# An attention and MLP kernel on one core: each attention unit's preparation written one unit ahead, with a third buffer slot for its loads

## The chip, the cores and the metric

The kernel runs on one core of a Trainium2 chip. The metric is the device time of one execution in microseconds (us). The engines are named as the profile names them: PE is TensorE (matmuls; PEld are its weight loads), DVE is VectorE, ACT is ScalarE, POOL is GpSimd, SP is SyncE, which computes nothing and issues every DMA of this kernel from one in-order queue.

## What is computed

Four batches, eight heads, 576 tokens, head width 64. Each head's output mixes causal softmax attention with a read from a memory matrix, and all heads together feed a two-layer MLP with a squared ReLU:

```python
scores = scale * np.matmul(q, k.transpose(0, 1, 3, 2))      # causal mask, softmax -> a
local = np.matmul(a, v)
q_p = np.where(q > 0, q, np.exp(q) - 1.0) + 1.0
mem_out = einsum(q_p, M_prev) / (einsum(q_p, z_prev)[..., None] + 1e-06)
x = g * mem_out + (1 - g) * local                            # (2304, 512)
r = np.maximum(x @ w_in, 0.0)                                # w_in (512, 2048)
return (r * r) @ w_out                                       # w_out (2048, 512)
```

## The kernel before

**Tiles and units.** The 576 tokens of a batch are one tile of 64 and four of 128 (tiles 1 to 4). Tile 0 of every batch is done first, by `first_tokens`. The rest is 24 attention units (line 999): a unit is a batch, a pair of heads and a list of tiles. Units 0 to 3 are tiles 1 and 2 of batch 0, units 4 to 7 its tiles 3 and 4; 8 to 11 and 12 to 15 are the same for batch 1; units 16 to 19 and 20 to 23 are all four tiles of batches 2 and 3. Within a unit the tiles go in the order 2, 1, 3, 4 (`TORD`).

**A unit's front** (lines 440 to 537). From three loads, `kd` (k), `qm` (the memory matrix and q) and `vv` (v), it makes, from unit 6 on, the high and low halves of q and k (`qh`, `ql`, `kh`, `kl`: ACT line 444 and 450, DVE 445 and 451, POOL for early `kl`); phi of q in place in `qm` (ACT 461 and 466, DVE 467); from unit 3 on, a power-of-two scale of v (`vx` line 483, a small matmul `vt` line 487, `vy`) and with it v's halves `vs` (ACT 498, DVE 500); and the memory products `pm` (PE 520), which DVE turns into the first part of the unit's output `feat` (531).

**A unit's rows** (lines 541 to 665). For each tile: scores `sp` (PE 554, three terms by two heads), masked minimum (DVE 575), exponential (ACT 595), the halves `a` of the weights (ACT 633, DVE 635), their transposition `aT` (a DMA on SP's queue, 639), the products with `vs` into `acc` (PE 659), and the scaled sum onto `feat` (DVE 662).

**Loads.** `loads` (414) allocates `kd`, `qm` and `vv` from tags with two buffers each (`KB`, `QB`, `VVB`). `after()`, called between a unit's front and its rows (539), loads the next unit. So a load is held until the unit two before has let go of its buffer.

**MLP blocks.** `moe(n)` for block 0 (the four 64-token tiles) and then for blocks of 256 tokens: block 1 and 2 are batch 0, 3 and 4 batch 1, 5 and 6 batch 2; the two of batch 3 go through `moe_last` at the end. A block is eight steps of 24 matmuls `up` (lines 936 to 938, 256 columns each), squared ReLU and halves (`r`, `gh`, `gl`: ACT 942 to 945, DVE 948) and 12 matmuls `oacc` (908 to 910, 512 columns each). It can start when the four units with its tiles have finished, and their tokens have been split (`hl`) and transposed into `xT` (DMA, 694).

**What sets the order.** The program text is written in the order of `ORD` (line 88): units 0 to 3 merged with the weights' conversion and MLP block 0, then units 4 to 23, then the other MLP blocks. A scheduler then lays the instructions out, engine by engine, and prefers what was written earlier among what it takes to be ready; MLP matmuls, written last, fill what attention leaves on PE. What comes out is a fixed in-order list for each engine. Tiles of one tag share that tag's buffers, and a PSUM tag (`av`, two buffers) is shared by `vt`, `pm` and `acc`.

Of the kernel before, what the change touches and what calls it, by code (L numbers as in the profile page):

```python
# [8 lines left out]
F32 = mybir.dt.float32  # L9
# [9 lines left out]
B, H, S, D = 4, 8, 576, 64  # L19
# [3 lines left out]
P = 128  # L23
# [6 lines left out]
SQ = S - D  # L30
# [11 lines left out]
NEF = 3  # L42
NES = 6
PXT = 'av'
PXE = 'aa'
PHI = 1
QB = 2
VVB = 2
ZW = D + 1
MW = 576  # L50
NRAW = 8
# [8 lines left out]
EB = 3  # L60
EB2 = 3
RB = 2
KB = 2
XB = 3
SEQ = 'a0 g a1 r r c0 l r r c1'
W0 = 9
# [2 lines left out]
NEARLY = 12  # L69
# [11 lines left out]
FIRST = 4  # L81
# [18 lines left out]
def fused_kernel(ctx: ExitStack, tc: tile.TileContext, t0_d, kk_d, qv_d, beta, w_in, w_out, out):  # L100
# [5 lines left out]
    at = atx.enter_context(tc.tile_pool(name="at", bufs=1, side="right"))  # L106
# [26 lines left out]
    def load_beta():  # L133
        nc.sync.dma_start(gpm, beta)
        gates()
# [123 lines left out]
    more = []  # L259
# [12 lines left out]
    def ahead():  # L272
        if len(loaded) < NU:
            load_weight(len(loaded))
            loaded.append(1)
# [16 lines left out]
    def weights():  # L292
        with tc.tile_pool(name="rw", bufs=1) as rw:
            more.append(rw)
            with tc.tile_pool(name="tp", bufs=1, reuse_waits="tile") as tp:
                first_tokens(tp, ahead)
            yield
            yield from pieces(0, NR0, NRAW)
        wpl.append(ctx.enter_context(tc.tile_pool(name="wpl2", bufs=1, reuse_waits="tile")))
        with tc.tile_pool(name="rw2", bufs=1, reuse_waits="tile") as rw:  # L300
            more.append(rw)
            yield from pieces(NR0, NU, NRAW2)
        more.append(ltx.enter_context(tc.tile_pool(name="late", bufs=1, reuse_waits="tile")))
        yield

    def first_tokens(tp, ahead):
# [8 lines left out]
        for step in SEQ.split():  # L315
            if step == "r":
                ahead()
            elif step == "l":
                nxt.append(loads(*order[0]))
            elif step == "g":  # L320
                load_beta()
            else:
                g = int(step[1])
                c0, c1 = {"a": (0, TA), "q": (0, GD), "k": (GD, TA), "c": (TA, TW)}[step[0]]
                nc.sync.dma_start(tr[g][:, c0:c1], t0_d[g, :, c0:c1])
# [85 lines left out]

    feat = {}

    def loads(b, p, tiles):
        qa, qb = QT[tiles[0]][0], sum(QT[tiles[-1]])
        kd = at.tile([P, S], F32, tag="kd", name="kd", bufs=KB)
        nc.sync.dma_start(kd[:, :qb], kk_d[b, p, :, :qb])
        qm = at.tile([P, 2 * ZW + SQ], F32, tag="qm", name="qm", bufs=QB)
        qa, qb = qa - D + 2 * ZW, qb - D + 2 * ZW
        for c0, c1 in [(0, qb)] if qa == 2 * ZW else [(0, 2 * ZW), (qa, qb)]:  # L420
            nc.sync.dma_start(qm[:, c0:c1], qv_d[b, p, :, c0:c1])
        vv = at.tile([P, 5 * P], F32, tag="vv", name="vv", bufs=VVB)
        nv = (tiles[-1] + 1) * P
        nc.sync.dma_start(vv[:, :nv], qv_d[b, p, :, SQ + 2 * ZW : SQ + 2 * ZW + nv])
        return kd, qm, vv

    def attention(b, p, tiles, ld, after, early, sfull, full, ap):
        q_eng, k_eng = (nc.gpsimd if c == 'p' else nc.vector for c in (EARLY if early else LATE))
        late = 0 if early else 1
        h0 = 2 * p  # L430
# [3 lines left out]
        kd, qm, vv = ld  # L434
# [102 lines left out]
            yield  # L537

        after()
        started, a12 = set(), None  # L540
        row = {}

# [43 lines left out]
        for i in [t for t in TORD if t in tiles]:  # L586
            q0, n = QT[i]
# [112 lines left out]
    def prefetch(b, blk):  # L700
        n = blocks.index((b, blk))
        if n < NBLK - 2:
            xT = mo.tile([P, 2, 2 * NK, P], F16, tag="xT", name="xT", bufs=2)
            osc = mo.tile([P, 2], F32, tag="osc", name="osc", bufs=2)
            xq[n] = xT, osc
            token_halves(b, blk, [xT[:, t] for t in range(2)], osc)
            return
# [279 lines left out]
    def need(n):  # L987
        while wn[0] < n:
            next(wg)
            wn[0] += 1  # L990
# [8 lines left out]
    order = []  # L999
# [3 lines left out]
    nxt = []  # L1003
    need(1)
    if not nxt:
        nxt.append(loads(*order[0]))

    def attn(i0, i1):
        for i in range(i0, i1):
            ld = nxt.pop()  # L1010

            def after():
                if i + 1 < len(order):
                    nxt.append(loads(*order[i + 1]))

            yield from attention(*order[i], ld, after, i < NEARLY, i < NES, i < NEF and max(order[i][2]) < 4, more[-1] if i > FIRST and i % 2 else at)
            b, p, tiles = order[i]
            if p == NP - 1:
                need(NU + 2)
                for blk in range(2):  # L1020
                    if 2 * blk + 1 in tiles and b < B - 1:
                        prefetch(b, blk)
                yield

    def na(t):
        return NP * (6 + (len(t) > 3) + 2 * len(t) - 1)

    ORD(merge, attn, na, wsteps, lambda: moe(0), order)
    tl = last_pool()
    for _ in chain(*[moe(n) for n in range(1, NBLK - 2)], moe_last(tl)):  # L1030
# [55 lines left out]
```

## Time and profile before

| what | us |
|---|---|
| median of 3 runs (lowest to highest) | 586.88 (583.03 to 589.49) |
| the profiled execution | 584.98 |
| its span, first to last instruction | 583.2 |
| PE busy in the span | 535.7 (92%) |
| DVE busy | 455.7 (78%) |
| ACT busy | 397.2 (68%) |
| SP's hardware DMA queue, share of 16 DMA engines | 50.6% |

The profile gives each engine's busy time, the idle time ahead of an instruction, and which event ended it. A PE instruction's duration holds its way through the array, so matmuls overlap and their cadence is read from start to start. Idle time of an engine that is not the bound costs nothing by itself.

### The profile page before, as it was taken

To read this page: it belongs to the slowest core of one execution; us is meant where nothing else is said; L and a number is where in the kernel's file an instruction comes from. 1 tells how busy PE (TensorE), PEld (TensorE's weight loads), DVE (VectorE), ACT (ScalarE), POOL (GpSimd) and SP (SyncE) were. 2 spreads that over 40 slices of the span, in tenths; PEclk is the share of its full clock that TensorE was granted. 3 is DMA by queue.
4 is the path that set the end of the run, shared out by engine and by line. 5 is a ranking of instruction groups with operands and counts; after the bars stand their busy time and mean duration, and the time that the engine had idled before them with its cause. 6 is when DMAs were issued, how large, how long until landed. Compare 5 with 4: busy or idle time off the path is not lost.

```text
span 583.2 us, 12895 instructions
## 1 busy us (share of the span) xinstructions
PE 535.7 (92%) x4903; PEld 380.4 (65%) x4903; DVE 455.7 (78%) x1413; ACT 397.2 (68%) x853; POOL 59.7 (10%) x41
## 2 busy tenths in 40 slices
PE   6578997799799899999998999988999999999997
PEld 6466774576577576657765766656676776446766
DVE  6988779998687686889895775989767769795735
ACT  2566886777688677869787866889566664556452
POOL 2760674010010000000000000000000000000000
PEclk9968998699999999999998999999999999999999
DMA  8921886345865643767546846569454335100002
GB/s 308 404 89 38 281 320 164 90 100 121 157 128 117 143 118 91 158 136 174 123 108 104 196 74 118 117 122 178 64 114 86 79 57 71 38 0 1 2 1 72
DMA packets 131022, 70.87 MB, mean 122 GB/s; under 512 B 113296, under 2 KB 119440, under 8 KB 130960
## 3 DMA queue, kind: packets, MB, share of 16 engines
q1 hardware_dynamic: 130960, 70.05, 50.6%
q8 instruction: 38, 0.62, 0.5%
q14 instruction: 24, 0.20, 0.1%
HBM read 37.53 MB, written 4.72 MB: 72 GB/s over the span
## 4 chain that ended last, share of the span: by engine, by line
PE 35%; DVE 21%; ACT 12%; DMA 10%; issue 4%; SPq 1%; POOLq 0%; DVEq 0%; ACTq 0%
DVE a L635 4%; PE oacc L909 4%; PE oacc L908 4%; PE oacc L910 4%; PE up L938 4%; PE up L936 4%; PE up L937 4%; DMA qm<-in_qv_dram 3%; DVE e L575 3%; ACT e L595 3%; DMA vv<-in_qv_dram 3%; PE seven L811 3%; DMA aT<-a 3%; PE acc L659 3%; PE sp L554 2%
## 5 line engine op out<-in xcount | busy, mean ns | idle before, releaser
L936 PE MATMUL up<-xT,w 128*128 128x256 f16 x448 | 123.1, 275 | 1.2 <-ACT r L942 1.2
L937 PE MATMUL up<-xT,w 128*128 128x256 f16 x448 | 123.1, 275 | 0.3 <-DVE xT L397 0.3
L938 PE MATMUL up<-xT,w 128*128 128x256 f16 x448 | 123.2, 275 | 0.0
L595 ACT ACTIVATE e<-e,mx 128x320 f32<-128x320 f32 (+3 forms) x128 | 77.4, 606 | 46.3 <-DVE feat L662 27.4
L908 PE MATMUL oacc<-w,gh 128*128 128x512 f16 x224 | 85.5, 382 | 2.2 <-ACT gh L945 2.1
L635 DVE SCALAR_TENSOR_TENSOR a<-e,a 128x128 f16<-128x128 f32 x116 | 64.8, 569 | 27.3 <-ACT a L633 26.4
L909 PE MATMUL oacc<-w,gh 128*128 128x512 f16 x224 | 85.4, 381 | 0.0
L910 PE MATMUL oacc<-w,gl 128*128 128x512 f16 x224 | 81.0, 380 | 1.3 <-DVE gl L948 1.2
L633 ACT ACTIVATE a<-e 128x128 f16<-128x128 f32 x116 | 54.9, 523 | 3.9 <-DMA aT<-a 2.4
L659 PE MATMUL acc<-vs,aT 128*128 128x64 f16 x1138 | 46.3, 195 | 11.7 <-DMA aT<-a 7.2
L659 PEld LDWEIGHTS <-aT 128*128 128x128 f16 x1138 | 41.5, 99 | 20.8 <-DMA aT<-a 10.2
L937 PEld LDWEIGHTS <-w 128*128 128x128 f16 x448 | 44.3, 99 | 11.5 <-issue 1.5
L938 PEld LDWEIGHTS <-w 128*128 128x128 f16 x448 | 44.2, 99 | 9.2 <-issue 1.2
L936 PEld LDWEIGHTS <-w 128*128 128x128 f16 x448 | 44.2, 99 | 9.2
L575 DVE CUSTOM_DVE_ANT_0 e<-sp,mask 128x320 f32<-128x320 f32 (+3 forms) x128 | 47.0, 417 | 1.5 <-PE sp L554 1.0
L193 POOL TENSOR_SCALAR raw<-raw 128x512 uint32<-128x512 uint16 x21 | 44.8, 2134 | 21.4 <-DMA raw<-in_w_in_dram 12.8
L948 DVE TENSOR_TENSOR gl<-r,gh 128x512 f16<-128x512 f32 x56 | 39.4, 704 | 7.3 <-ACT gh L945 6.9
L942 ACT ACTIVATE r<-up,gam 128x512 f32<-128x512 f32 x48 | 32.3, 674 | 18.2 <-PE up L938 18.2
L910 PEld LDWEIGHTS <-gl 128*128 128x128 f16 x224 | 21.4, 98 | 23.5 <-DVE gl L948 3.4
L811 PEld LDWEIGHTS <-g 128*128 128x128 f16 x336 | 32.6, 98 | 6.0 <-DVE g L737 1.8
L908 PEld LDWEIGHTS <-gh 128*128 128x128 f16 x224 | 22.0, 98 | 22.1 <-ACT gh L945 2.7
L943 ACT ACTIVATE r<-r 128x512 f32<-128x512 f32 x56 | 34.9, 624 | 0.8
(196 smaller groups left out, 1076.1 us busy)
## 6 DMA issues: line engine op xcount, KB each, us to landing
raw<-in_w_in_dram SPq DMA_DIRECT2D x16, 512.0 KB, 7.1
raw<-in_w_out_dram SPq DMA_DIRECT2D x16, 512.0 KB, 7.9
vv<-in_qv_dram SPq DMA_DIRECT2D x16, 320.0 KB, 3.2
kd<-in_kk_dram SPq DMA_DIRECT2D x16, 288.0 KB, 3.2
out_dram<-o SPq DMA_DIRECT2D x12, 256.0 KB, 2.4
qm<-in_qv_dram SPq DMA_DIRECT2D x8, 321.0 KB, 3.4
qm<-in_qv_dram SPq DMA_DIRECT2D x8, 193.0 KB, 2.9
vv<-in_qv_dram SPq DMA_DIRECT2D x8, 192.0 KB, 4.7
```

Of the source, the lines that this page charges most:

```text
L575: nc.vector.tensor_tensor_reduce(out=e[:, h, ka:kb], in0=sps[:, h, cs], in1=mask[:, 448 - q0 + ka : 448 - q0 + kb], scale=-0.125, scalar=3 ...
L595: ex = nc.scalar.activation(e[:n, h, :ke], e[:n, h, :ke], AF.Exp, bias=bs, scale=-1.0, accum_out=sm[:n, h : h + 1])
L633: nc.scalar.mul(av[:, :, o0 : o0 + w], x, SC)
L635: nc.vector.scalar_tensor_tensor(out=av[:, :, o0 + w : o0 + 2 * w], in0=x, scalar=SC, in1=av[:, :, o0 : o0 + w], op0=ALU.mult, op1=ALU.sub ...
L659: nc.tensor.matmul(acc[:n, h], lhs[:, :n], rhs, start=x == 0, stop=x == len(mms) - 1)
L811: mms.append(nc.tensor.matmul(x[:, blk], g[j][:, i0, a, blk, p], t_side(j, p, m, i1), start=j == js[0] and p == n == 0, stop=j == js[-1] a ...
L908: nc.tensor.matmul(acc[t], gh[:, u, ts], w_out_op(f, 0), start=f == f0, stop=False)
L909: nc.tensor.matmul(acc[t], gh[:, u, ts], w_out_op(f, 1), start=False, stop=False)
L910: nc.tensor.matmul(acc[t], gl[:, u, ts], w_out_op(f, 0), start=False, stop=f == f1)
L936: nc.tensor.matmul(up[:, u, :], w_in_op(f, k, 0), xT[:, :, k], start=k == 0, stop=False)
L937: nc.tensor.matmul(up[:, u, :], w_in_op(f, k, 0), xT[:, :, NK + k], start=False, stop=False)
L938: nc.tensor.matmul(up[:, u, :], w_in_op(f, k, 1), xT[:, :, k], start=False, stop=k == NK - 1)
```

## The change

Nothing is computed otherwise; every engine has the same instructions. Three things move.

First, `attention` gets a stop: after a unit's front and its `after()` it yields the word `whole`. `attn` now writes, from unit `FIRST` = 4 on, the front of unit i+1 ahead of the rows of unit i. Second, `loads` names its buffers by slot: unit i uses slot i mod 2 below unit 8 (`AHEAD`) and i mod 3 from there on, each slot its own tag with one buffer; the third slot lies in the pool `more[-1]`. Third, `after()` of unit i loads up to unit i+1, and from unit 6 on up to unit i+2.

```diff
-QB = 2
-VVB = 2
-KB = 2
+AHEAD = 8
-    def loads(b, p, tiles):
+    def loads(i):
+        b, p, tiles = order[i]
+        n = i % 2 if i < AHEAD else i % 3
+        lp = at if n < 2 else more[-1]
-        kd = at.tile([P, S], F32, tag="kd", name="kd", bufs=KB)
+        kd = lp.tile([P, S], F32, tag=f"kd{n}", name="kd")
-        qm = at.tile([P, 2 * ZW + SQ], F32, tag="qm", name="qm", bufs=QB)
+        qm = lp.tile([P, 2 * ZW + SQ], F32, tag=f"qm{n}", name="qm")
-        vv = at.tile([P, 5 * P], F32, tag="vv", name="vv", bufs=VVB)
+        vv = lp.tile([P, 5 * P], F32, tag=f"vv{n}", name="vv")
...
         after()
+        if ap_early:
+            yield "whole"
...
+    def unit(i):
+        ld = nxt.pop(0)
+        def after():
+            while i + len(nxt) + 1 < min(len(order), i + (3 if i + 2 >= AHEAD else 2)):
+                nxt.append(loads(i + len(nxt) + 1))
+        ap = more[-1] if i > FIRST and i % 2 else at
+        early = i < NEF and max(order[i][2]) < 4
+        return attention(*order[i], ld, after, i < NEARLY, i < NES, early, ap, i >= FIRST)
     def attn(i0, i1):
+        ahead = []
         for i in range(i0, i1):
-            ld = nxt.pop()
-            def after():
-                if i + 1 < len(order):
-                    nxt.append(loads(*order[i + 1]))
-            yield from attention(*order[i], ld, after, i < NEARLY, i < NES, i < NEF and max(order[i][2]) < 4, more[-1] if i > FIRST and i % 2 else at)
+            rows = ahead.pop() if ahead else unit(i)
+            if i >= FIRST:
+                for x in (rows,) if i == FIRST else ():
+                    for _ in iter(lambda: next(x), "whole"):
+                        yield
+                if i + 1 < i1:
+                    ahead.append(unit(i + 1))
+                    for _ in iter(lambda: next(ahead[0]), "whole"):
+                        yield
+            yield from rows
```

What the scheduler makes of it is shown at two places; names carry the program's numbers, which differ between the two kernels, and the changed kernel's lines are 2 or 4 apart from the old ones.

SP's queue around the load of unit 11's `qm` and `vv`, before. Here `qm_2495` and `vv_2497` are unit 11's, `aT_2410` is unit 9's and `aT_2525` unit 10's transposition, `kd_2894` is unit 14's:

```order
L639 DMA_TRANSPOSE aT_2410<-a_2409 128x6x128
L417 DMA kd_2894<-in_kk_dram 128x576
L639 DMA_TRANSPOSE aT_2525<-a_2524 128x10x128
L421 DMA qm_2495<-in_qv_dram 128x386
L639 DMA_TRANSPOSE aT_2525<-a_2524 128x6x128
L424 DMA vv_2497<-in_qv_dram 128x384
```

The same two loads now, as `qm_2311` and `vv_2313`; `aT_2217` is unit 7's last transposition, `aT_2341` is unit 8's, `kd_2656` is unit 13's:

```order
L643 DMA_TRANSPOSE aT_2217<-a_2216 128x18x128
L643 DMA_TRANSPOSE aT_2341<-a_2340 128x10x128
L643 DMA_TRANSPOSE aT_2341<-a_2340 128x6x128
L423 DMA qm_2311<-in_qv_dram 128x386
L426 DMA vv_2313<-in_qv_dram 128x384
L419 DMA kd_2656<-in_kk_dram 128x576
```

Unit 11's q and v stood among unit 10's transpositions; they now stand behind unit 8's, two units earlier. The loads of units 12 to 23 have moved by one to two units in the same way.

PE around the first `up` matmul of MLP block 5 (the first block of batch 2, which needs tiles 1 and 2 of units 16 to 19), before. `oacc_6371` is block 4's last sum, the two `pm` are unit 20's memory products, `up_6666` is the new block's first tile:

```order
L910 LDWEIGHTS gl_6631
L910 MATMUL oacc_6371<-w31_1407,gl_6631 128x512
L520 MATMUL pm_4326<-qm_4071 128x130 x2
L520 MATMUL pm_4333<-qm_4071 128x130 x2
L936 LDWEIGHTS w0_522
L936 MATMUL up_6666<-xT_4260,w0_522 128x256
```

And now, where `up_6604` is a step of block 4:

```order
L941 MATMUL up_6604<-xT_3366,w27_1354 128x256
L942 LDWEIGHTS w27_1354
L942 MATMUL up_6604<-xT_3366,w27_1354 128x256
L940 LDWEIGHTS w0_522
L940 MATMUL up_6666<-xT_4314,w0_522 128x256
```

Before, block 4 had run out, down to its last `oacc`, when block 5 began; between unit 19's last product of tile 1 and this matmul PE had 7 `up` and 24 `oacc` matmuls. Now block 4 still has steps to go, and between the same two points stand 96 `up` and 37 `oacc` matmuls.

## Rows read from the trace of the kernel before

**Rows 1.** Busy time by stretch: length, then PE, PEld, DVE, ACT, POOL, clock, DMA.

```profile
134.00:480.00 346.00, 327.10 (x3199) 232.76 (x3197) 269.00 (x966) 255.51 (x585) 3.93 (x4) 1.00 0.60 121
165.00:279.00 114.00, 108.61 (x1024) 77.03 (x1022) 90.38 (x323) 87.29 (x204) 1.87 (x2) 1.00 0.63 137
279.00:441.00 162.00, 152.78 (x1506) 108.98 (x1506) 126.27 (x470) 123.22 (x284) 0.00 (x0) 0.99 0.61 118
480.00:573.00 93.00, 92.04 (x597) 57.91 (x596) 65.39 (x93) 48.32 (x62) 0.00 (x0) 1.00 0.10 18
```

**Rows 2.** Waits of PE, 134 to 480: us in total, times, longest.

```profile
PE acc L659 <- DMA aT<-a: 7.2, 5, 2.8
PE sp L554 <- DVE ql L445: 3.0, 3, 2.3
PE up L936 <- ACT r L942: 1.0, 1, 1.0
```

**Rows 3.** Timeline, unit 11's q: start, us, instruction, and idle before with releaser.

```profile
196.54 0.61 PE L520 MATMUL pm<-qm 128*128 128x130 f32 x4
...
199.49 0.65 SPq L421 DMA_DIRECT2D qm<-in_qv_dram  x1
...
203.43 0.41 PE L554 MATMUL sp<-kh,qh 64*128 64x320 f32 x2 [2.30 <-DVE ql L445]
```

**Rows 4.** Timeline of PE, start to start of neighbouring matmuls.

```profile
377.39 0.27 PE L938 MATMUL up<-xT,w 128*128 128x256 f16 x1
377.50 0.38 PE L908 MATMUL oacc<-w,gh 128*128 128x512 f16 x1
377.72 0.38 PE L909 MATMUL oacc<-w,gh 128*128 128x512 f16 x1
```

**Rows 5.** Timeline of PE, where it stood idle, and unit 17's tile 3.

```profile
147.34 0.99 PE L659 MATMUL acc<-vs,aT 128*128 128x64 f16 x28 [1.22 <-DMA aT<-a]
...
156.85 0.20 PE L659 MATMUL acc<-vs,aT 128*128 128x64 f16 x1 [1.89 <-DMA aT<-a]
...
312.49 1.73 PE L659 MATMUL acc<-vs,aT 128*128 128x64 f16 x29 [2.75 <-DMA aT<-a]
...
335.55 1.62 PE L659 MATMUL acc<-vs,aT 128*128 128x64 f16 x50
...
384.68 0.39 PE L908 MATMUL oacc<-w,gh 128*128 128x512 f16 x1 [1.57 <-ACT gh L945]
...
386.47 0.22 PE L487 MATMUL vt<-identb,vx 128*128 128x128 bf16 x1 [0.74 <-DVE feat L662]
...
405.67 0.99 PE L659 MATMUL acc<-vs,aT 128*128 128x64 f16 x28 [1.57 <-DVE mx L575]
...
450.97 1.63 PE L659 MATMUL acc<-vs,aT 128*128 128x64 f16 x50 [1.16 <-DMA aT<-a]
```

**Rows 6.** SP's transposition for unit 17's tile 3, and all transpositions of line 639.

```profile
330.44 1.51 SPq L639 DMA_TRANSPOSE aT<-a  x1
...
DMA to landing us min/median/max: 2.7/4.1/6.7
```

**Rows 7.** Waits of DVE, 279 to 441.

```profile
DVE vx L483 <- DMA vv<-in_qv_dram: 7.9, 4, 3.0
```

**Rows 8.** Timeline: block 2's tokens on SP, and the block's first `up` on PE.

```profile
186.99 2.72 SPq L694 DMA_TRANSPOSE xT<-hl  x2
...
193.78 0.27 PE L936 MATMUL up<-xT,w 128*128 128x256 f16 x1
```

**Rows 9.** Waits of DVE, 165 to 279.

```profile
DVE ql L445 <- ACT qh L444: 5.2, 4, 2.0
DVE vx L483 <- DMA vv<-in_qv_dram: 4.8, 5, 1.4
```

**Rows 10.** Timeline: unit 10's transposition on SP, and its products on PE.

```profile
198.07 1.33 SPq L639 DMA_TRANSPOSE aT<-a  x1
...
213.53 0.22 PE L659 MATMUL acc<-vs,aT 128*128 128x64 f16 x2
```

More of the change, by code (lines that the diff above doesn't have):

```diff
@@ L318, in first_tokens @@
             elif step == "l":
-                nxt.append(loads(*order[0]))
+                nxt.append(loads(0))
             elif step == "g":
@@ L425, in loads, with attention @@
         return kd, qm, vv
-    def attention(b, p, tiles, ld, after, early, sfull, full, ap):
+    def attention(b, p, tiles, ld, after, early, sfull, full, ap, ap_early):
         q_eng, k_eng = (nc.gpsimd if c == 'p' else nc.vector for c in (EARLY if early else LATE))
@@ L1005, in fused_kernel @@
     if not nxt:
-        nxt.append(loads(*order[0]))
+        nxt.append(loads(0))
+    def unit(i):
[6 more added lines that the diff above has]
+        return attention(*order[i], ld, after, i < NEARLY, i < NES, early, ap, i >= FIRST)
     def attn(i0, i1):
+        ahead = []
         for i in range(i0, i1):
-            ld = nxt.pop()
-            def after():
-                if i + 1 < len(order):
-                    nxt.append(loads(*order[i + 1]))
-            yield from attention(*order[i], ld, after, i < NEARLY, i < NES, i < NEF and max(order[i][2]) < 4, more[-1] if i > FIRST and i % 2 else at)
+            rows = ahead.pop() if ahead else unit(i)
[8 more added lines that the diff above has]
+            yield from rows
             b, p, tiles = order[i]
```

## The prediction

> **What bounds the kernel now.** I read the busy time by stretch first. From 134 us on, when attention units 4 to 23 and the MLP blocks run together, to 480 us, when only MLP is left, PE is busy for 327.1 of 346 us; behind that, for 92.0 of 93 [rows 1]. PE is the bound. Its work is the same before and after, and so is the start, where the order is unchanged until unit 5's `vt`. So the change can only win or lose PE's idle time: there are 18.9 us of it between 134 and 480, and 1 us in the tail. A shorter attention chain is worth nothing in itself, since MLP matmuls fill PE meanwhile.
>
> Then the waits of PE, to see what that idle time is. The largest kind is products that wait for a transposition (7.2 us in five waits), then scores that wait for `ql` (3.0 in three) [rows 2]. The timeline around the longest of the second kind shows its cause: unit 9's memory products end at about 197 and free its `qm`; SP issues unit 11's `qm` into it at 199.49; the scores of unit 11 start at 203.43, after 2.30 us of idle PE [rows 3]. That is the two-buffer wait which the change is about. It is small on PE. It is larger on the engines that prepare: DVE stood 5.2 us for the `qh` that hangs on `qm` and 4.8 us for `vv` between 165 and 279, and 7.9 us for `vv` between 279 and 441 [rows 7, 9].
>
> **The change part by part.** The sum is made against the profiled execution, 584.98 us, which is 1.9 below the median of the three runs shown. No instruction is added or removed, and the same loads are issued on the same queue. I price moves by PE's cadence: an `up` matmul follows its neighbour by 0.11 us and an `oacc` matmul by 0.22 [rows 4]; how many of them stand between two points is counted in the old and the new instruction order. Scores, products and `pm` between the points differ little and are left out.
>
> *Loads two units earlier.* In the new order unit 11's `qm` stands behind unit 8's transpositions instead of among unit 10's, and its buffer is the one that unit 8 left. The scores' waits for `ql` have no reason left: -3.0 [rows 2]. Ends: 0 if another wait takes their place at once, -3.0.
>
> *Units 5 and 6.* PE stood 1.22 and 1.89 us for the transpositions of unit 5's last tile and unit 6's first [rows 5]. Between unit 5's last scores and those products there were 42 `up` and 12 `oacc` matmuls, now 40 and 31, which is 4.0 us more cover; for unit 6, 51 and 13, now 74 and 36, 7.6 us more. Both gaps are covered twice over: -3.1. Unit 5's front now waits in front of unit 4's products on PE, but unit 5's loads are in place by then, and 4.0 us are the price only if they were not.
>
> *MLP block 5.* At 384.68 and 386.47 PE stood 1.57 and 0.74 us, and 1.0 us more at the start of block 5 [rows 2, 5]. Here block 4 had run out of `up` matmuls, and block 5 could not start until unit 19 was done, so nothing hid the squared ReLU of block 4's last step. Attention now leads block 5 by 96 `up` and 37 `oacc` matmuls instead of 7 and 24, 12.7 us more: -3.3. Ends: -3.3, or -1.6 if only the first of the three goes.
>
> *Unit 20's last tile.* It stood 1.57 us at 405.67 [rows 5]. From the scores of unit 20's tile 4 to its products of tiles 3 and 4 the order had 81 and 8 matmuls, now 62 and 36, 4.1 us more: -1.6.
>
> *What comes out shorter.* The same count from a unit's scores of tile 4 to its products of tile 3 has shrunk in units 17, 18, 19, 21 and 22: from 64 and 28 to 48 and 26, from 51 and 33 to 54 and 21, from 48 and 33 to 52 and 26, from 57 and 35 to 45 and 24, and from 44 and 24 to 48 and 16. By the cadence these are 2.2, 2.3, 1.1, 3.7 and 1.3 us, 10.6 in all. There is little to take them from. Tile 3's transposition stands behind tile 4's on SP: unit 17's is issued at 330.44, lands 4.1 us later by the median, at 334.5, and its products start at 335.55, so 1.0 us is to spare [rows 5, 6]; unit 22 has nothing and already waits 1.16 [rows 5]. With 1.0 to spare in the four others, 6.6 us of new waits are left. Against that stand the 7.9 us that DVE no longer waits for `vv` in this stretch [rows 7], about half of it ahead of the weights of these five units. I take +3. Ends: 0 and +6.6. Unit 16's wait of 2.75 stays, its count is 57 and 36 before, 59 and 36 now.
>
> *MLP block 2.* Its tokens' second transposition is issued at about 188.3 and lands near 192.4 (with the same 4.1); the block starts at 193.78, 1.4 us later [rows 6, 8]. Units 4 to 7 now finish later against PE: from unit 7's last product to the block's first matmul there were 66 and 28 matmuls, now 38 and 24, 4.0 us less. 4.0 - 1.4 = 2.6, of which something is given back because the splitting of the tokens also moves; +2. Ends: 0 and +2.6.
>
> *A denser stretch.* This is the dearest unknown. From unit 8's first scores (165 us) to unit 16's (279 us) the old order holds 368 `up` and 188 `oacc` matmuls, the new one 282 and 144: 19.1 us of MLP work has gone to the tail, and attention must do the same work in 114 - 19.1 = 94.9 us if PE is not to wait more than now. DVE is busy 90.4 us in the old stretch [rows 1], 95% of 94.9 (the few steps' `gl` that leave it are left out). Its idle time is 23.6 us now; the two waits on loads, 10.0 us, go [rows 9], and 13.6 would remain. 90.4 + 13.6 = 104.0, 9.1 over. But these units have room: unit 10's transposition is issued at 198.07, lands near 202.2, and its products start at 213.53, 11 us later [rows 6, 10], so part of the lag is taken out of that. +3, between 0 and +9.1.
>
> Sum: 585.0 - 3.0 - 3.1 - 3.3 - 1.6 + 3 + 2 + 3 = 582.0 us.
>
> A rule speaks for more. The Trainium skill, Perfetto Trace Analysis, section Optimization Strategy, says that a gap which keeps coming back on the engine that should be saturated can mean that buffers are too few for the next tile. By it all 7.2 us of transposition waits would be buffer waits too and go with the third slot, and the sum would be 569.9. The rows agree for the scores' waits alone: the transpositions wait for DVE's weights and for SP's queue, and the third slot holds loads only.
>
> **The rivals.** *The gaps go and nothing comes for them.* The last three terms are 0: 585.0 - 11.0 = 574; with unit 16's and 22's waits gone too, 570. For it speaks that DVE and ACT lose their waits on loads, which shortens every chain behind them; against it, unit 17's margin of 1.0 us.
>
> *DVE becomes the bound of units 8 to 15; slower than before.* If DVE's busy share in this stretch stays at 90.4/114 = 0.79, it takes the 114 us it took, 19.1 over the 94.9, in place of the +3: 598. The point from which it decides: the other terms sum to -6.0, so beyond 100.9 us, a share under 0.90, the change loses. For it speaks that the share must rise at all while PE was the pacemaker; against it, that 10 of the 23.6 idle us have a cause that the change removes.
>
> *Loads in the transpositions' way; slower.* Loads are now issued closer behind transpositions. If landing moves from the median of 4.1 to the longest seen, 6.7 [rows 6], the eight four-tile units, with at most 1 us of margin, wait 1.6 to 2.6 us more each: some +13 on units 16 to 23, 595. The Trainium skill, Trainium Kernel Development and Optimization, section Key Constraints, says that all queues share the same 16 DMA engines and interleave there. Against it: the stretch's DMA share is 0.61 [rows 1] and the bytes are the same.
>
> *No effect.* Waits change places and PE's idle time stays: 585.
>
> **How the numbers follow.** My forecast, 582 with a range of its own of 577 to 588: 0.40. Gaps go: 0.27. DVE bound: 0.18. Loads in the way: 0.05. No effect: 0.10. About 1% (5.9 us) is what a measurement of this kernel can tell from no change. Faster by more, below 579: all of the second case and a quarter of the first, 0.37. Slower by more, above 591: most of the two slow cases, 0.17. Within: 0.46. The range of 8 in 10 goes from 570, the low end of the second case, to 593, short of the two slow cases' 595 and 598.
>
> **What would show it.** Right: no wait of scores for `ql`, none of `vx` or `qh` for a load, from unit 8 on; the waits at block 5 gone; attention's last product earlier by more than 10 us while the end moves by 3; waits for `aT` at tile 3 of units 17 to 22. Wrong: DVE's share in units 8 to 15 under 0.90 with PE idle there (third case), or no `aT` waits in units 16 to 23 (second case). Most likely to be wrong are the last three terms, 8 us that rest on chains which the trace shows only under other pacing.

## The result, and the profile after

The changed kernel takes 575.4 us (median, 574.6 to 576.0) against 585.5 (583.0 to 589.5) for the kernel before, measured beside it: a ratio of 0.987, with a 95% interval of 0.983 to 0.992. In a later group of runs, beside other kernels, it was 577.6 against 583.7, 0.988 (0.983 to 0.993). So it is faster by 1.2 to 1.3%. Ratios leave out executions that ran more than 1.5% above the fastest of their kernel. The forecast was 582 with a range of 570 to 593; the time lies inside that range, but 6.6 us below its point, in the gap between the forecast's own case (577 to 588) and the rival in which the gaps go and nothing comes for them (570 to 574); the second measurement lies in the forecast's own case. The profiled executions are 584.98 before and 575.25 after, 9.7 us apart; their spans are 583.2 and 573.5.

Busy time by stretch of the changed kernel (columns as in [rows 1]; units 8 to 15 now lie between 165 and 258 us):

```profile
134.00:480.00 346.00, 332.33 (x3286) 236.39 (x3285) 287.75 (x997) 261.25 (x591) 6.15 (x5) 1.00 0.62 123
165.00:258.00 93.00, 88.95 (x894) 64.05 (x894) 83.47 (x321) 77.74 (x189) 2.00 (x2) 1.00 0.79 159
```

PE stands idle for 13.7 us between 134 and 480, where it was 18.9 [rows 1]. Units 8 to 15 take 92.9 us from first scores to first scores (165.2 to 258.1) in place of 113.7, with DVE busy for 83.5 of 93 us, a share of 0.90 where it was 0.79. Attention's last product is at 446 us; it was at 473.

The waits of PE in the same 346 us (us in total, times, longest), to set against [rows 2]:

```profile
PE acc L663 <- DMA aT<-a: 5.4, 6, 1.5
PE up L940 <- DMA xT<-hl: 2.6, 1, 2.6
PE sp L558 <- DVE nm L527: 1.9, 1, 1.9
PE oacc L912 <- ACT gh L949: 1.9, 2, 1.3
```

The scores' wait for `ql` is gone; the waits of the products (`acc`) for transpositions have fallen from 7.2 to 5.4 us; a wait of block 2 for its tokens and one of 1.9 us on DVE are new. The larger change is on the engines that prepare. ACT and DVE, 134 to 480, waits on loads, before:

```profile
ACT qh L444 <- DMA qm<-in_qv_dram: 20.8, 12, 2.9
DVE vx L483 <- DMA vv<-in_qv_dram: 16.8, 11, 3.0
```

and after:

```profile
ACT qh L446 <- DMA qm<-in_qv_dram: 1.8, 2, 1.5
DVE vx L485 <- DMA vv<-in_qv_dram: 0.8, 1, 0.8
```

37.6 us of waiting for q, the memory matrix and v have become 2.6. Where PE still stands (timeline of PE, idle time and what ended it in brackets):

```profile
165.19 0.41 PE L558 MATMUL sp<-kh,qh 64*128 64x320 f32 x2 [1.87 <-DVE nm L527]
...
195.78 0.27 PE L940 MATMUL up<-xT,w 128*128 128x256 f16 x1 [2.61 <-DMA xT<-hl]
...
261.39 0.39 PE L912 MATMUL oacc<-w,gh 128*128 128x512 f16 x1 [1.25 <-ACT gh L949]
...
296.98 1.19 PE L663 MATMUL acc<-vs,aT 128*128 128x64 f16 x35 [0.27 <-DMA aT<-a]
...
337.61 0.58 PE L663 MATMUL acc<-vs,aT 128*128 128x64 f16 x14 [0.75 <-DMA aT<-a]
...
371.78 0.39 PE L912 MATMUL oacc<-w,gh 128*128 128x512 f16 x1 [0.61 <-ACT gh L949]
...
387.33 0.99 PE L663 MATMUL acc<-vs,aT 128*128 128x64 f16 x28 [1.30 <-DMA aT<-a]
...
407.78 0.70 PE L663 MATMUL acc<-vs,aT 128*128 128x64 f16 x18 [1.51 <-DMA aT<-a]
...
427.98 0.70 PE L663 MATMUL acc<-vs,aT 128*128 128x64 f16 x18 [1.18 <-DMA aT<-a]
```

These are, in order: unit 8's first scores, the start of MLP block 2, an MLP step that waits for its `gh`, the products of tiles 3 and 4 of units 16 and 18 (tile 3's come first), a step of block 4 (not its last: 23 of the block's `up` matmuls still follow), tile 4 of unit 20, and tiles 3 and 4 of units 21 and 22. Unit 17 waits 0.41 us at 317.06. A row that begins with a wait can show fewer matmuls than the run that follows it.

The kernel before shows one more thing that the prediction had overlooked. At 312.49 PE had stood 2.75 us for unit 16's tile 3 [rows 5]. Busy time by stretch just behind it, kernel before; the third number from the end is the granted clock:

```profile
312.00:314.00 2.00, 1.51 (x29) 1.51 (x30) 1.46 (x9) 0.00 (x0) 0.00 (x0) 0.58 1.01 214
314.00:316.00 2.00, 2.00 (x32) 1.80 (x30) 0.83 (x4) 1.58 (x5) 0.00 (x0) 0.57 0.15 28
```

The clock of TensorE stood for part of these stretches at 1.2 GHz, the lower of its two levels. Over the two stretches of 4 us from 310 to 318 the granted clock is 0.79 and 0.78, so (0.21 + 0.22) x 4 = 1.7 us of work at full speed was lost on top of the idle time. It is the only such fall between 134 and 480 in the kernel before; in the changed one no 4 us of that time are under 0.97.

### The profile page after: what moved, and what is told of

It reads as the page before. It is cut to its first block, busy times and chain, and to the rows that moved or that the text cites. A ratio compares the mean times of both kernels' runs of the same rounds, so it can differ in the third digit from the quotient of the medians.

```text
span 573.5 us, 12883 instructions
## 1 busy us (share of the span) xinstructions
PE 531.8 (93%) x4903; PEld 378.3 (66%) x4903; DVE 456.3 (80%) x1413; ACT 398.1 (69%) x853; POOL 60.1 (10%) x41
## 4 chain that ended last, share of the span: by engine, by line
PE 32%; DVE 29%; ACT 12%; DMA 7%; issue 4%; SPq 0%; ACTq 0%; DVEq 0%
DVE a L639 6%; DVE e L579 6%; DMA aT<-a 4%; ACT e L599 4%; PE seven L815 4%; PE up L940 3%; PE up L941 3%; PE up L942 3%; PE oacc L913 3%; PE oacc L912 3%; PE oacc L914 3%; ACT a L637 3%; PE seven L788 2%; PE seven L786 2%; PE seven L787 2%
## 5 line engine op out<-in xcount | busy, mean ns | idle before, releaser
L940 PEld LDWEIGHTS <-w 128*128 128x128 f16 x448 | 44.3, 99 | 11.3 <-DMA xT<-hl 0.5
L663 PE MATMUL acc<-vs,aT 128*128 128x64 f16 x1138 | 41.8, 193 | 7.8 <-DMA aT<-a 5.4
L663 PEld LDWEIGHTS <-aT 128*128 128x128 f16 x1138 | 38.6, 98 | 15.4 <-DMA aT<-a 7.7
L191 POOL TENSOR_SCALAR raw<-raw 128x512 uint32<-128x512 uint16 x21 | 45.0, 2141 | 19.8 <-DMA raw<-in_w_in_dram 10.4
L946 ACT ACTIVATE r<-up,gam 128x512 f32<-128x512 f32 x48 | 32.2, 673 | 14.8 <-PE up L942 12.3
```

The lines of the kernel that those rows point to most:

```text
L663: nc.tensor.matmul(acc[:n, h], lhs[:, :n], rhs, start=x == 0, stop=x == len(mms) - 1)
L940: nc.tensor.matmul(up[:, u, :], w_in_op(f, k, 0), xT[:, :, k], start=k == 0, stop=False)
```

## The experiments

All ratios are to the kernel before, measured on the same chip in the same group of runs; it took 584.3, 583.7, 583.9 and 584.8 us in the four groups of the experiments. Times from different groups are compared below without a correction for this. "Falls" counts the places between 134 and 478 us of the profiled execution where the granted clock of a 4 us stretch goes under 0.97 (neighbouring stretches are one place); it is a count in one execution of each kernel. The two columns of waits are ACT's for `qm` at the line of `qh`, and DVE's for `vv`, 134 to 480 us.

| kernel | us | ratio (95%) | qm | vv | falls |
|---|---|---|---|---|---|
| before | 585.5 | 1 | 20.8 | 16.8 | 1 |
| changed | 575.4 | 0.987 (0.983 to 0.992) | 1.8 | 0.8 | 0 |
| changed, again | 577.6 | 0.988 (0.983 to 0.993) | 0.4 | 0.7 | 0 |
| written ahead, two slots | 592.4 | 1.016 (1.011 to 1.021) | 15.7 | 14.5 | 3 |
| third slot alone | 580.3 | 0.995 (0.992 to 0.997) | 12.3 | 0 | 2 |
| ahead from unit 16 | 583.3 | 1.000 (0.997 to 1.002) | 12.4 | 0 | 2 |
| ahead from unit 8 | 578.8 | 0.990 (0.987 to 0.994) | 7.0 | 4.0 | 1 |
| third buffer for vv alone | 582.9 | 0.998 (0.995 to 1.001) | 8.7 | 0.9 | 1 |
| changed, tile 3 first | 577.8 | 0.990 (0.985 to 0.994) | 3.1 | 0.8 | 0 |
| before, tile 3 first | 583.4 | 1.001 (0.998 to 1.004) | 20.7 | 13.2 | 3 |
| loads from POOL | 603.0 | 1.032 (1.028 to 1.037) | 15.5 | 12.8 | 4 |
| fourth buffer for kd, qm; tile 3 first | 581.0 | 0.995 (0.992 to 0.997) | 1.4 | 2.9 | 1 |

### The two parts apart

Two slots, and loads one unit ahead; fronts still written ahead:

```diff
-AHEAD = 8
+AHEAD = 99
```

> The changed kernel without its third slot: loads two slots and one unit ahead in all units, the writing ahead from unit 4 kept. Theory A (the gain is a set of named waits of PE, the third slot takes the waits for ql and vv, the writing ahead takes those at units 5 and 6 and at block 5): the waits of scores for ql come back, some 3 us, the one of 2.6 at block 2 stays; 578. Theory B (the third slot is the whole gain): 583 to 585, with DVE waiting for vv some 12 us as before. Theory C (the writing ahead is the whole gain, because a front written early lets go of the load buffers early too): 575, no wait for ql.

592.4 us: slower than all three theories said, and 8.1 slower than the kernel before in its group (584.3). Scores wait for `ql` nowhere, as theory C had it, but that is not where the cost lies. Timeline of this kernel around unit 16's load, DVE:

```profile
257.96 0.82 DVE L485 TENSOR_REDUCE vx<-vv 128x1 f32<-128x640 f32 x1 [4.05 <-DMA vv<-in_qv_dram]
...
259.36 1.15 DVE L639 SCALAR_TENSOR_TENSOR a<-e,a 128x128 f16<-128x128 f32 x2
```

ACT, the same kernel and place:

```profile
257.15 0.62 ACT L446 CAST qh<-qm 128x512 fp32r<-128x512 f32 x1 [1.81 <-DMA qm<-in_qv_dram]
...
258.21 1.03 ACT L637 ACTIVATE a<-e 128x128 f16<-128x128 f32 x2
259.14 0.60 ACT L949 CAST gh<-r 128x512 f16<-128x512 f32 x1
```

and PE:

```profile
259.80 0.39 PE L912 MATMUL oacc<-w,gh 128*128 128x512 f16 x1 [2.26 <-ACT gh L949]
```

DVE stands 4.05 us for unit 16's `vv`, and behind it in DVE's list are weights (`a`) of the units whose rows are under way. ACT stands 1.81 us for the same unit's `qm`, and behind that are weights and the half `gh` of an MLP step, for which PE then stands 2.26 us. In the kernel before the loads were as late (DVE waited 16.8 us for `vv` there, 14.5 here), but the front that waits for them stood behind the last unit's rows. So a front that is written ahead takes its wait for a load with it, in front of work that PE needs soon. The three falls of the clock, behind waits for transpositions at 312.3, 406.4 to 408.8 and 451.7, cost, by the granted clock of the six stretches concerned, (0.11 + 0.32 + 0.16 + 0.27 + 0.11 + 0.31) x 4 = 5.1 us more.

The third slot alone, loads two units ahead, no front written ahead:

```diff
-        return attention(*order[i], ld, after, i < NEARLY, i < NES, early, ap, i >= FIRST)
+        return attention(*order[i], ld, after, i < NEARLY, i < NES, early, ap, 99 <= i < 99)
...
-            if i >= FIRST:
+            if 99 <= i < 99:
```

> The third slot and the loads two units ahead kept, no front written ahead of the last unit's rows. Theory A: no wait for ql or vv; by the order, the matmuls ahead of block 2 are again 57 up and 36 oacc, so its 2.6 us go; unit 5's 1.2 us come back (46 and 10), unit 6's do not (70 and 24); block 5 has 48 and 24 in place of 7 and 24 before, so its waits stay away; 574. Theory B: 575. Theory C: 584 to 585.

580.3 us, 0.995 of the kernel before: a gain, but under half of the changed kernel's, so theories A and B are both short by 5 to 6 us, and theory C (584 to 585) is 4 us too high. By place theory A was right: no wait at block 2, none at block 5, none for `vv`. What it left out stands elsewhere. Timeline of PE:

```profile
255.08 0.31 PE L663 MATMUL acc<-vs,aT 128*128 128x64 f16 x2 [2.59 <-ACT vs L500]
...
399.54 0.29 PE L663 MATMUL acc<-vs,aT 128*128 128x64 f16 x2 [3.36 <-DMA aT<-a]
```

Unit 13's products now wait for their own v's halves, which are made late because the front stands behind the last unit's rows; unit 20's last tile waits 3.36 us where the changed kernel waits 1.30. Behind both the clock falls, by (0.16 + 0.27) x 4 = 1.7 and (0.24 + 0.50 + 0.11) x 4 = 3.4 us. Together 2.59 + 3.36 - 1.30 + 5.1 = 9.8 us; the changed kernel has 2.61 at block 2 and 1.87 at unit 8 that this one has not. 9.8 - 4.5 = 5.3, and the two spans differ by 4.1 (577.6 and 573.5), so these waits are enough to explain the difference; that nothing else bears on it is not shown.

So the two parts do not add: -0.5% alone, +1.6% alone, -1.3% together.

### Writing ahead from a later unit on

From unit 16 (the same flag with `16 <= i < 99`), and from unit 8 (`8 <= i < 99`):

> The third slot kept, fronts written ahead only from unit 16 on. Theory A, by the matmuls that the order has at each place: 3.3 us at block 5 come back (7 up and 16 oacc ahead of it), 1.2 at unit 5 come back, 2.6 at block 2 go; 577. Theory B: 575. Theory C: 580, half of the gain.

> The third slot kept, fronts written ahead only from unit 8 on. Theory A: unit 5's 1.2 us come back, block 2's 2.6 go (57 up and 48 oacc ahead of it), block 5 is covered (83 and 40); 574, faster than the changed kernel. Theory B: 575. Theory C: 576 to 577, a fifth of the gain lost.

From unit 16: 583.3 us, the place right and the sum wrong. With 7 `up` and 16 `oacc` matmuls ahead of block 5 its waits are back, as theory A said. Timeline of PE:

```profile
384.55 0.39 PE L912 MATMUL oacc<-w,gh 128*128 128x512 f16 x1 [1.79 <-ACT gh L949]
...
386.01 0.22 PE L489 MATMUL vt<-identb,vx 128*128 128x128 bf16 x1 [0.42 <-DVE feat L666]
...
387.78 0.27 PE L940 MATMUL up<-xT,w 128*128 128x256 f16 x1 [0.67 <-DMA xT<-hl]
```

These are 2.9 us of the 3.3 that the kernel before had there. But it shares unit 13's wait for its v's halves with the kernel above (up to unit 16 the two are the same), and unit 17 waits 2.15 us for a transposition at 335.53, with a fall of the clock behind each.

From unit 8: block 2's wait is gone and block 5 is covered, as expected, and still it takes 578.8 us, no faster than the changed kernel (0.990 against 0.987 and 0.988, with overlapping intervals). What block 2 no longer costs comes back at unit 10, whose products wait 1.63 us at 213.03 with a fall of the clock behind it, and in a wait of 2.58 us at 345.04.

### Which buffer of the three

A third buffer for `vv` only; `kd` and `qm` have two:

```diff
-        lp = at if n < 2 else more[-1]
-        kd = lp.tile([P, S], F32, tag=f"kd{n}", name="kd")
-        qm = lp.tile([P, 2 * ZW + SQ], F32, tag=f"qm{n}", name="qm")
-        vv = lp.tile([P, 5 * P], F32, tag=f"vv{n}", name="vv")
+        lp, lv, m = at, at if n < 2 else more[-1], i % 2
+        kd = lp.tile([P, S], F32, tag=f"kd{m}", name="kd")
+        qm = lp.tile([P, 2 * ZW + SQ], F32, tag=f"qm{m}", name="qm")
+        vv = lv.tile([P, 5 * P], F32, tag=f"vv{n}", name="vv")
```

> The changed kernel once more, beside the kernels of this group on one chip. 575 if the first measurement holds; 577 or more would mean that part of its lead over the variant that writes ahead from unit 8 on (578.8) is the chip's or the day's.

> The changed kernel with a third buffer for vv alone; kd and qm have two again. The kernel with two slots throughout took 592, 8 more than before, and DVE waited 14.5 us for vv in it. Theory D (a front that is written ahead puts DVE's wait for vv into its in-order queue in front of the last unit's weights; this is what the third slot takes away): the wait for vv goes, 575 to 578. Rival S (what costs is SP's queue, where a load of qm or kd that is held by its buffer stands in front of transpositions; SP waited 17.6 us at the loads of qm and 24 at those of kd): 586 to 592.

582.9 us, between the two theories; the changed kernel in the same group took 577.6. DVE's wait for `vv` fell from 14.5 to 0.9 us, and 9.4 of the 14.8 us by which the two-slot kernel is slower than the changed one went with it (this kernel also loads two units ahead, where that one loads one, and the two-slot kernel is from another group of runs). ACT still waits 8.7 us for `qm`, and PE again stands for `gh` behind such a wait: 3.6 us in three waits, where the changed kernel has 1.7 in two. So the third buffer for `vv` and the earlier loads are the larger part; that `qm` is the whole of the rest is likely by this wait, and not shown.

### What holds tile 3's transposition

The prediction had put the waits for `aT` in units 16 to 23 down to SP's queue, where tile 3's transposition stands behind tile 4's. One line holds it ahead:

```diff
-                nc.sync.dma_start_transpose(out=aT[:, :, :n], in_=a[:n])
+                tr = nc.sync.dma_start_transpose(out=aT[:, :, :n], in_=a[:n]); last3.append(tr) if i == 3 else [tc.add_manual_dep(tr.ins, x.ins.name, AFTER, reason="tile 3 first") for x in last3 if i == 4]
```

> The changed kernel with one thing more: the transposition of a unit's tile 3 is held ahead of that of tile 4 on SP's queue. In units 16 to 23 it stands behind it now, and unit 16's weights of tile 3, ready at 279.6 us, are issued at 292.8. Theory T (this place in the queue is what is left of PE's waits for aT, 5.4 us in six): they go, 570 to 572. Rival (tile 4 lands later by what tile 3 gains, or the waits come from DVE's weights): 575.

> The kernel before with that one thing alone. Theory T: the waits at unit 16 (2.75), 20 (1.57) and 22 (1.16) go, 579 to 581. Rival: 584 to 586; the wait of unit 16 came from late weights.

577.8 us against 577.6, and 583.4 against 583.7: no effect on the time in either kernel. Theory T falls, and the first half of its rival holds: tile 4 lands later by what tile 3 gains. Timeline of the changed kernel with tile 3 first, at unit 16, and PE at unit 17's products of tile 4 (28 matmuls; tile 3 has 22):

```profile
280.29 0.94 DVE L639 SCALAR_TENSOR_TENSOR a<-e,a 128x768 f16<-128x768 f32 x1
...
291.13 0.92 PE L663 MATMUL acc<-vs,aT 128*128 128x64 f16 x26
...
292.08 1.52 SPq L643 DMA_TRANSPOSE aT<-a  x1
...
322.61 0.99 PE L663 MATMUL acc<-vs,aT 128*128 128x64 f16 x28 [1.60 <-DMA aT<-a]
```

and a wait of SP in the same kernel, 270 to 300 us:

```profile
SPq L643 <- PE acc L663: 3.3, 1, 3.3
```

Tile 3's weights are done at 281.2; its transposition goes out at 292.08, right behind unit 16's products of tiles 2 and 1 (the 26 matmuls that begin at 291.13). The code has the reason: `TAGS = [0, 16, 16, 16, 18]` gives tiles 1, 2 and 3 one tag, and so one buffer `aT16` (line 624 makes it of the width `tg`). Tile 3's transposition cannot start before the products of tiles 2 and 1 have read theirs, and with tile 3 first, tile 4's now stands behind it. So the wait has passed to tile 4's products: PE waits for `aT` for 5.7 us in eight places, seven of them tile 4's, where the changed kernel has 5.4 in six. In the kernel before, the same edit takes away most of unit 16's wait (2.75 becomes 1.06) and gives unit 17 one that it did not have. With tile 3 first, SP there issues unit 17's tile 3 behind tile 1's products and tile 4's behind that, which the kernel before had issued at 325.20:

```profile
330.15 1.60 SPq L639 DMA_TRANSPOSE aT<-a  x1
...
331.80 3.34 SPq L639 DMA_TRANSPOSE aT<-a  x1
...
338.72 0.99 PE L659 MATMUL acc<-vs,aT 128*128 128x64 f16 x28 [2.61 <-DMA aT<-a]
```

In all, PE waits 11.0 us in ten places for `aT` in the kernel before with this edit, and 7.2 in five without; the execution with the edit that was profiled is the slowest of its twelve (587.0).

Without the edit, tile 3's transposition is held by one of two things. In the kernel before it is `aT16` for units 17 to 21, whose tile 3 goes out 0.2 us after the last product of tile 1 has begun. Unit 17's products of tile 1 are at

```profile
329.95 0.46 PE L659 MATMUL acc<-vs,aT 128*128 128x64 f16 x10
```

and SP issues its tile 3 at 330.44 [rows 6], 2.0 us after the end of tile 4's transposition. So the prediction's reading that tile 4's place on SP holds it there was wrong. In units 16, 18, 21 and 22 of the changed kernel it is tile 4's transposition, which itself goes out as soon as tile 4's weights are done; tile 3's follows it, 1.8 to 4.2 us after the last product of tile 1 has begun. Unit 21 of the changed kernel:

```profile
398.86 0.92 PE L663 MATMUL acc<-vs,aT 128*128 128x64 f16 x26
...
399.01 1.21 DVE L639 SCALAR_TENSOR_TENSOR a<-e,a 128x1024 f16<-128x1024 f32 x1
...
400.25 2.81 SPq L643 DMA_TRANSPOSE aT<-a  x1
...
403.23 1.95 SPq L643 DMA_TRANSPOSE aT<-a  x1
```

The products of tiles 1 and 2 are through at 399.8, tile 4's weights at 400.22; tile 4's transposition goes out at 400.25 and tile 3's right behind it, at 403.23. PE starts the products of both at 407.78. So two transpositions, one after the other on SP, have to land before PE can do both tiles, whichever goes first. What covers them is what PE has between a unit's products of tile 1 and those of tile 3: in units 16 to 23 the orders hold 4.2 to 5.9 us of MLP matmuls there in the changed kernel and 3.4 to 6.2 in the kernel before (at 0.11 and 0.22 us each). Whether a buffer of its own for tile 3, whose transposition could then go out long before tile 4's, would take these waits away was not tried.

### Loads from another queue, and a fourth buffer

In the run above a load of `qm` held SP's queue for 10.4 us ahead of unit 16's transposition. To see whether such loads are in the way, those of units 8 to 23 were issued from POOL's queue:

```diff
-        n = i % 2 if i < AHEAD else i % 3
-        nc.sync.dma_start(kd[:, :qb], kk_d[b, p, :, :qb])
+        n = i % 2 if i < AHEAD else i % 3; ld = nc.gpsimd if i >= AHEAD else nc.sync
+        ld.dma_start(kd[:, :qb], kk_d[b, p, :, :qb])
```

(`qm` and `vv` alike), then the same with two slots, and with tile 3 first.

> The changed kernel with the loads of units 8 to 23 issued from POOL's queue in place of SP's; buffers, order of the fronts and everything else as in the changed kernel. Holding tile 3 ahead of tile 4 on SP did not bring unit 16's transposition forward: it was still issued at 292.1 us, 10.9 after its weights, behind a load of qm that waited 10.4 us for its buffer. Theory S (what is left of the waits for aT, and the 2.7 us at block 2, come from loads that are held on SP's queue in front of transpositions): both go, 569 to 572. Rival (the transpositions are late for other reasons, or loads from POOL land later): 575 to 580.

> Two slots throughout and fronts written ahead (the kernel that took 592), with the loads of units 8 to 23 issued from POOL's queue. The third buffer for vv alone gave 583, so 9 of its 15 us over the changed kernel went with DVE's wait for vv, and 5 did not. Theory D (DVE's wait for a late vv, in front of the last unit's weights, costs most; a held load still waits for its buffer on any queue): 583 to 590, with 10 us or more of DVE waiting for vv. Theory S (late vv is itself made by SP's queue, where loads stand behind transpositions and transpositions behind held loads): 572 to 578, with the waits for vv under 4 us.

> The changed kernel with the loads of units 8 to 23 from POOL's queue, and tile 3's transposition held ahead of tile 4's on SP. Theory S with T (once no load is in the way, the order of the two transpositions decides): PE's waits for aT, 5.5 us in the changed kernel, fall under 2; 567 to 571, and faster than with the loads moved alone. Rival: the same as with the loads moved alone.

603.0, 629.1 and 616.0 us, ratios of 1.032, 1.067 and 1.045: all three far outside of every expectation, and no test of theory S, because the loads now come late for reasons of POOL's own. Timeline of POOL in the first of them, three loads, of which nothing holds the last two:

```profile
111.81 0.55 POOL L419 DMA_DIRECT2D kd<-in_kk_dram  x1 [7.13 <-DVE fc L196]
114.63 0.54 POOL L423 DMA_DIRECT2D qm<-in_qv_dram  x1 [2.26 <-issue]
117.59 0.54 POOL L426 DMA_DIRECT2D vv<-in_qv_dram  x1 [2.42 <-issue]
```

and SP's queue in the changed kernel, the same three loads:

```profile
122.56 0.57 SPq L419 DMA_DIRECT2D kd<-in_kk_dram  x1
123.19 0.43 SPq L423 DMA_DIRECT2D qm<-in_qv_dram  x1
123.66 0.43 SPq L426 DMA_DIRECT2D vv<-in_qv_dram  x1
```

2.8 and 3.0 us from start to start on POOL against 0.5 to 0.6 on SP; between 134 and 480 us POOL stands 53.3 us ahead of 17 loads without a releaser, 3.1 each. Its list also has loads behind the early `kl`, which wait 20.6 us for ACT's `kh` in three places, and behind loads held for a buffer; how much each of these costs was not separated. Loads come late (15.5 us of ACT waiting for `qm`, 12.8 of DVE for `vv`), and with fronts written ahead that costs as it did with two slots: PE stands 6.7 us in two waits at `pm` and 4.6 in two for `r`, where the changed kernel has none and 0.4, and the clock falls in four places. The Trainium skill, Trainium Kernel Development and Optimization, section Key Constraints, says that issuing DMAs from several engines at once only saves the sequencer's time to issue; here, by the rows above, a load that left SP freed 0.5 to 0.6 us there and took some 3 us of POOL.

The last run took the other way: SP issues, and `kd` and `qm` have four buffers from unit 8 on (`n, m = (i % 2,) * 2 if i < AHEAD else (i % 4, i % 3)`, with m for `vv`), tile 3 first.

> The kernel with tile 3's transposition held ahead of tile 4's (577.8), with a fourth buffer for kd and qm from unit 8 on; vv keeps three, and the loads are still issued two units ahead on SP, which issues one in about half a us (POOL took some 3 us for each, so the two runs with loads on POOL did not try this question). Theory S with T (a load of qm that is held for its buffer stands in front of tile 3's transposition): SP's waits at loads for a buffer, 23 us at qm in the changed kernel, fall under 5, unit 16's transposition is issued within 2 us of its weights, PE's waits for aT fall from 5.7 us to under 2.5; 572 to 574. Rival (the loads are held, but the products of tile 3 would come no earlier, since other work on SP or the matmuls' order holds them): 576 to 579, waits for aT as before.

581.0 us (577.2 to 584.2; the profiled execution is the fastest of the twelve, 577.2). Theory S with T did not come true as stated: SP's waits at loads of `qm` are still 15.8 us in two, since the order now places loads still earlier on SP (unit 20's `qm` ahead of unit 16's transposition), and the waits for `aT` are 7.5 us in five. So no run has the loads out of the way; what the trace says of them is told with the rivals below. Block 2's wait is gone in this run, but a wait of 2.90 us at 433.91, with a fall of the clock behind it, takes that back. Why the other executions are up to 7 us longer than the profiled one stays open. No variant was faster than the changed kernel.

## Why the prediction was right or wrong, point by point

**What bounds the kernel.** Right: PE is the bound, its work is the same, and the change wins PE's idle time. Incomplete: a stall of PE can also cost clock. The prediction priced each wait at its idle time; unit 16's cost 2.75 + 1.7 us.

**Loads two units earlier, -3.0.** Right, and the mechanism with it: no scores wait for `ql`, and the waits of ACT and DVE on loads went from 37.6 to 2.6 us. What was not seen is that this part carries the other: without the third slot the writing ahead loses 8 us in place of gaining.

**Units 5 and 6, -3.1.** Right; both waits are gone. In the kernels that write ahead only from a later unit, unit 5's tile has 0.8 us of another wait in that place.

**MLP block 5, -3.3.** Right: all three waits are gone. A step of block 4 now waits 0.61 us at 371.78, so -2.7 in size. Writing ahead from unit 16 only brought back 2.9.

**Unit 20's last tile, -1.6.** Wrong: 1.30 us is left. The step that failed is the count of matmuls from the scores of tile 4 to the products of tiles 3 and 4, 4.1 us more. It takes the weights for what is late. They were done in time, tile 3's at 371.0 and tile 4's at 379.6, and the last product of tile 1 began at 378.6; but SP was issuing two transpositions of MLP tokens (`xT`) until 380.2, tile 3's went out behind them and tile 4's behind that:

```profile
377.55 2.62 SPq L698 DMA_TRANSPOSE xT<-hl  x2
...
380.33 1.51 SPq L643 DMA_TRANSPOSE aT<-a  x1
...
381.97 3.39 SPq L643 DMA_TRANSPOSE aT<-a  x1
```

PE's products of tile 4 began at 387.33. What counted here is SP's queue.

**What comes out shorter, +3.** Right in size for the units named: new waits are 0.41 us in unit 17, 0.75 in 18 and 1.51 in 21, 2.7 together, in the three whose counts had shrunk most, and none in 19; unit 22 waits 1.18 us, as it did (1.16). Wrong for unit 16, whose 2.75 us were said to stay: 0.27 is left. In the kernel before, unit 16's weights of tile 4 came late, so SP issued tile 4 at 304.60, 2.3 us behind the end of the products of tile 1 (302.3), and tile 3 behind that; the changed kernel has tile 4's weights before these products end, and issues tile 4 at 290.05, 0.2 us ahead of their end at 290.3. SP, kernel before:

```profile
304.60 4.64 SPq L639 DMA_TRANSPOSE aT<-a  x2
```

and after:

```profile
290.05 4.32 SPq L643 DMA_TRANSPOSE aT<-a  x2
```

That is -2.5 of idle time and -1.7 of clock that no term had.

**MLP block 2, +2.** Right, at the upper end of its bounds: 2.61. In the kernels that have 14 to 17 us of matmuls in that place instead of 9.5 (third slot alone, ahead from 16, ahead from 8) the wait is not there.

**A denser stretch, +3.** Wrong, to the good side: 92.9 us, 2 under the 94.9 at which PE waits no more than before; PE is idle for 4.1 us of it (5.4 before). The failing step held 13.6 us of DVE's idle time fixed; it fell to 9.5 in all. And the few `gl` that had left the stretch were left out: 16 of them before, 11.3 us, and 11 after, 7.4 us, 3.9 us less for DVE to do. DVE's share came out at 0.90, the very point that the rival named; the 1.87 us for which unit 8's first scores wait on DVE, just ahead of this stretch, and 1.25 us for a `gh` behind it at 261.39 may belong to it, which no run shows.

**The rivals.** The time came near to the rival in which the gaps go (570 to 574 named, 575.4 measured), but not by its mechanism: its sign, no `aT` waits in units 16 to 23, did not show (5.4 us in six), and block 2 and unit 8 brought 4.5 us of new waits. DVE as the bound of units 8 to 15 did not come. Loads in the transpositions' way did not come either: transpositions land in 4.3 us by the median and 6.5 at most (4.1 and 6.7 before). SP was held for 10.3 us at a load of `qm` ahead of unit 16's transposition, but only until 281.18; the transposition goes out at 290.05, when tile 4's weights are done (290.02). Of the sign "none of `vx` or `qh` for a load", 2.6 of 37.6 us are left.

**The sum.** From the profiled 584.98: `ql` -3.0, units 5 and 6 -3.1, unit 16 -4.2, block 5 -2.7, unit 20 -0.3, block 2 +2.6, unit 8 +1.9, units 17, 18 and 21 +2.7: -6.1. Measured -9.7. By the two profiles, PE's idle time fell from 47.5 to 41.7 us (span less busy time) and its busy time for the same 4903 matmuls from 535.7 to 531.8. Of the 5.8 us of idle time the list has 4.4; the rest is the balance of smaller waits, such as one of unit 15's scores that went (1.16), a `gl` that went (1.00) and the `gh` that came (1.25). Of the 3.9 us of busy time 1.7 are the clock, and why the other 2.2 went stays open. The first 134 us give little: PE is idle for 23.9 of them before and 23.6 after. The forecast's point, 582.0, lies 6.7 us above the profiled execution: unit 16 is 4.2 of it, which no term had, the three terms of what comes for the gaps 0.8 (+7.2 in place of +8) and the open part 3.6; unit 20 (1.3) and block 5 (0.6) go the other way. That the three terms came out so near in sum is luck in part, since the third one stood for something that did not happen.

The rule of the Trainium skill on gaps that come back (Perfetto Trace Analysis, Optimization Strategy), by which the waits for transpositions were buffer waits too and the sum was 569.9, is not borne out: with the third slot there are 5.4 us of such waits, where there were 7.2. Another buffer than those that the change adds, `aT16`, does hold tile 3's transposition in some units, but in units 16, 18, 21 and 22 of the changed kernel it is free before the transposition goes out, and by the trace DVE's weights and SP's queue hold it, as the prediction said against the rule.

## What to carry to other kernels

Writing the next unit's preparation ahead pays only where its loads are already there; otherwise its wait for a load moves in front of work that is needed sooner, and the two edits have to be measured together (-0.5% and +1.6% apart, -1.3% as one). When a transfer goes out long after its data are ready, look up both what stands ahead of it in the queue and who last reads the buffer that it writes to, before the order of the queue is changed. Price a stall of PE at its idle time and, at the upper end, with the clock that the rows behind similar stalls show.

## What the runs showed of the hardware

The clock fell to its lower level behind some stalls of PE and not behind others: behind 2.75 us of idle time at 312.49 in the kernel before (1.7 us lost), behind 1.63 at 213.03 in the kernel that writes ahead from unit 8, and in the two-slot kernel three times, here behind a stall of 2.57 us at 451.67:

```profile
448.00:452.00 4.00, 1.43 (x24) 1.28 (x24) 2.59 (x8) 3.38 (x11) 0.00 (x0) 1.00 0.80 171
452.00:456.00 4.00, 4.00 (x59) 3.14 (x56) 2.58 (x15) 1.41 (x4) 0.00 (x0) 0.64 0.64 122
456.00:460.00 4.00, 4.00 (x37) 2.24 (x36) 1.69 (x3) 2.75 (x5) 0.00 (x0) 0.94 0.00 0
```

It did not fall behind 2.61 us at 195.78 in the changed kernel, nor behind 2.75 us at 196.83 in the same with tile 3 first, nor behind 2.30 at 203.43 in the kernel before. The same wait of unit 11's scores, 2.35 us at 203.13 in the kernel before with tile 3 first, was followed by a fall (granted clock 0.66 from 202 to 206). The length of the idle time alone does not tell which it will be. From one load to the next, with nothing in the profile that it waited for, POOL took 2.8 and 3.0 us and SP 0.5 to 0.6. A transposition of tile 4's weights kept SP for 2.5 to 4.2 us and one of tile 3's for 1.5 to 2.7 (units 16 to 23 of the two kernels), and the next on SP began behind it.
